# Sign of a weight through a parametric relu on ScalarE, a last value chunk on all rows, and a planner that knows TensorE's low clock

## The chip, the cores and the metric

The kernel runs on one core of one Trainium2 chip. The metric is the device time of one execution in microseconds (us), lower is better. TensorE is called PE here, VectorE DVE, ScalarE ACT, GpSimd POOL, and SyncE, which issues the DMAs, SP.

## What is computed

A masked attention over 4 batches, 8 heads, 576 positions and head size 64, then two layers of an MLP (2304 tokens, 512 to 2048 to 512):

```python
scores = scale * np.matmul(q, k.transpose(0, 1, 3, 2))
thresh = np.max(scores, axis=-1, keepdims=True) - tau
scores = np.where(scores >= thresh, scores, -1000000000.0)
attn = np.exp(scores - np.max(scores, axis=-1, keepdims=True))
attn = attn / (np.sum(attn, axis=-1, keepdims=True) + 1e-09)
x = np.matmul(attn, v)                      # then (2304, 512)
h = x @ w_in
x = (np.maximum(h, 0) + np.log1p(np.exp(-np.abs(h)))) @ w_out      # first MLP
h = x @ w_in2
out = (np.maximum(h, 0) ** 2) @ w_out2                             # second MLP
```

## The kernel before

**Stages.** The attention is cut into 32 units (`u`): two heads and half of the queries each. Four units give the 512 features of one group of 288 tokens; there are 8 groups. The first MLP works on one group at a time in 8 steps (`p`), each with 256 of the 2048 inner features; the second MLP works on 512 tokens at a time (`p` again 0 to 7). The first MLP begins when the first four units are done and runs beside the attention of the later ones; the second MLP follows.

**One unit.** `a_prep` splits q and k into a high and a low part (ACT, then POOL lines 250 and 251). `a_scores` makes the scores transposed, five chunks of 128 keys: four chunks with two heads side by side on 64 rows of PE each (line 266), the fifth with both heads' last 64 keys on 128 rows (line 271); ACT moves them to SBUF (line 274). `a_max` reduces them on DVE (lines 282 to 290) and spreads the maximum by a DMA to DRAM and back (292, 293). `a_soft` subtracts, masks (DVE, lines 300 and 302) and takes the exponential (ACT, line 303). `a_out` multiplies with the values on PE: for each of two heads four chunks on all 128 rows (line 314) and the last chunk on that head's 64 rows only (line 315); the chunk tensor `vp` has zeros in the rows of the other head. Each of these fp32 matmuls is two MATMUL records in the trace. ACT copies the results (316, 317), DVE divides (319 to 322). `x_split` splits the group's features (328, 329).

**MLP.** `m1_up` (lines 338 to 340, three matmuls per product on 288 columns), the softplus on ACT and DVE (348 to 351), a split (356, 357), `m1_down` (369 to 371). The second MLP has the same lines 338 to 340 and then 458 to 466 and 478 to 480.

**Weights.** They come as 64-bit floats: 64 pieces of 128x512 words, 32 for each MLP, in `Weights.load`. ACT scales the high word into `t` (line 227), which loses nothing but the sign; POOL multiplies the high word by zero, which leaves the sign bit (228); DVE shifts the low word and ors that sign in (229), then shifts `t` by three and ors (230); ACT rounds to the high part (231); POOL subtracts for the low part (232). The first MLP's 32 pieces have two buffers (`wraw`, `wt`), the second's three, and a buffer is loaded again when its last reader is done.

**Order.** Nothing is issued in the order of the code: `Plan` collects operations with an engine, an assumed duration, reads, writes and a key (the due step), and `emit` lists them by a simple model in which each engine takes the ready operation with the lowest key, operations with `lock=True` exclude POOL's, and costs such as a DMA's rate are constants of the class. That list is what each engine then executes strictly in order. One plan covers the attention with the first MLP, a second one the rest.

Of the kernel before, what the change touches and what calls it, by code (L numbers as in the profile page):

```python
# [12 lines left out]
AF = mybir.ActivationFunctionType  # L13
ALU = mybir.AluOpType
# [12 lines left out]
LAG = 13  # L27
EARLY = 6
PREPDVE = 1
WLEAD, W2LAG = 7, 3  # L30
GPOOL = range(8, 56)
DOWN = 2.0 ** -20


def f32(ap):
    return ap.bitcast(F32)


class Plan:
# [5 lines left out]

    SYNC, AFTER_PE, DRAIN, DMA_START, DMA_END, BYTES_PER_NS = 200, 300, 130, 1600, 950, 350

# [19 lines left out]
    def emit(self):  # L67
# [14 lines left out]
        future, ready, events = {}, {}, []  # L82
# [15 lines left out]
        while left:  # L98
# [10 lines left out]
            while future[e] and future[e][0][0] <= t:  # L109
                _, key, i = heapq.heappop(future[e])  # L110
                heapq.heappush(ready[e], (key, i))
            _, i = heapq.heappop(ready[e])
            eng, ns, fn, deps, key, nbytes, lock = self.ops[i]
# [27 lines left out]
def kernel(ctx: ExitStack, tc: tile.TileContext, qT, kT, vp, tau, w1i, w1o, w2i, w2o, out):  # L141
# [59 lines left out]


    class Weights:
        def __init__(self, pool, n):
# [6 lines left out]
        def load(self, src, f, outw, key=None):  # L211
            s = self.i % self.n
            self.i += 1
            raw, t = self.raw[s], self.t[s]
            R, T = ("wraw", id(self), s), ("wt", id(self), s)
            p, j = divmod(f, 2)
            hi, lo = (woh, wol) if outw else (wih, wil)
            W = ("wo" if outw else "wi", p)
            if outw:
                P.add("SP", 600, lambda: SP.dma_start(raw.rearrange("p e w -> p (e w)"), src[f * 128:(f + 1) * 128, :]), [], [R], key, 1 << 19)  # L220
                hf, lf, t2 = hi[p][:, j], lo[p][:, j], t
            else:
                P.add("SP", 600, lambda: SP.dma_start(raw.rearrange("p e w -> p (e w)"), src[f]), [], [R], key, 1 << 19)
                hf, lf = (x[p][:, :, 128 * j:128 * j + 128] for x in (hi, lo))
                t2 = t.rearrange("p (k f) -> p k f", k=4)
            low, high = raw[:, :, 0], raw[:, :, 1]
            P.add("ACT", 510, lambda: ACT.mul(f32(t), f32(high), 2.0 ** -112), [R], [T], key)
            P.add("POOL", 620, lambda: POOL.tensor_scalar(f32(high), f32(high), 0.0, 1.0, op0=ALU.mult, op1=ALU.mult), [], [R], key)
            P.add("DVE", 620, lambda: DVE.scalar_tensor_tensor(out=low, in0=low, scalar=29, in1=high, op0=ALU.logical_shift_right, op1=ALU.bitwise_or), [], [R], key, lock=True)  # L229
            P.add("DVE", 620, lambda: DVE.scalar_tensor_tensor(out=t, in0=t, scalar=3, in1=low, op0=ALU.logical_shift_left, op1=ALU.bitwise_or), [R], [T], key, lock=True)  # L230
            P.add("ACT", 510, lambda: ACT.copy(hf, f32(t2)), [T], [W], key)
            P.add("POOL", 1230, lambda: POOL.tensor_tensor(lf, f32(t2), f32(hf), op=ALU.subtract), [T], [W], key)

# [19 lines left out]
    def a_scores(u, key):  # L253

        st, ST = st_t[u % 3], ("st", u % 3)
        half = [slice(0, 64), slice(64, 128)]
        ops = [(k_h, q_h), (k_l, q_h), (k_h, q_l)]
        QK = ["k_h", "k_l", "q_h", "q_l"]
        for c in range(5):
            banks = [(y_ps[i], ("y", i)) for i in (2 * (c % 2), 2 * (c % 2) + 1)] if u < EARLY else [(a_ps[i], ("a", i)) for i in range(2)]  # L260
            cs = slice(128 * c, 128 * c + 128)
            if c < 4:
                def mms(banks=banks, cs=cs):
                    for n, (k, q) in enumerate(ops):
                        for o in range(2):
                            PE.matmul(banks[o][0][:, :HALF], k[half[o], cs], q[half[o]], start=(n == 0), stop=(n == 2))  # L266
                P.add("PE", 590, mms, QK, [b[1] for b in banks], key + 0.1 * c)
            else:
# [7 lines left out]
    def a_max(u, key):  # L276
# [10 lines left out]
        for a in range(4):  # L287
            P.add("DVE", 175, lambda a=a: DVE.tensor_copy(mr[:, 1 + a, :18], r[32 * a:32 * a + 32].rearrange("p o b -> p (o b)")), [R], [MR], key)
        P.add("DVE", 360, lambda: DVE.tensor_reduce(mr[:, 0, :18], mr[:, 1:5, :18].rearrange("p a x -> p x a"), axis=AX.X, op=ALU.max), [], [MR], key)
# [14 lines left out]

    def a_out(u, key):
        e, E = st_t[u % 3], ("st", u % 3)
        vt, V = v_t[u % 2], ("v", u % 2)
# [3 lines left out]
        for o in range(2):  # L311
            bank, BK = a_ps[o][:, :HALF], ("a", o)
            for c in range(4):
                P.add("PE", 486, lambda c=c, o=o, bank=bank: PE.matmul(bank, vt[:, 192 * c + 64 * o:192 * c + 64 * o + 128], e[:, 5 * o + c], start=(c == 0), stop=False), [E, V], [BK], key + o)  # L314
            P.add("PE", 486, lambda o=o, bank=bank: PE.matmul(bank, vt[half[o], 768 + 128 * o:896 + 128 * o], e[half[o], 4], start=False, stop=True), [E, V], [BK], key + o)  # L315
            P.add("ACT", 310, lambda o=o, bank=bank: ACT.copy(xf[half[o]], bank[half[o]]), [BK], [XF], key + o - 0.5)
# [15 lines left out]
    def up(banks, p, xh, xl, X, ns, key):  # L332

        for j, (bank, BK) in enumerate(banks):
            f = slice(128 * j, 128 * j + 128)
            for c in range(4):
                def mms(bank=bank, c=c, f=f):
                    PE.matmul(bank, wih[p][:, c, f], xh[c], start=(c == 0), stop=False)  # L338
                    PE.matmul(bank, wih[p][:, c, f], xl[c], start=False, stop=False)  # L339
                    PE.matmul(bank, wil[p][:, c, f], xh[c], start=False, stop=(c == 3))  # L340
                P.add("PE", 3 * ns, mms, [("wi", p)] + X(c), [BK], key)

# [16 lines left out]
    def m1_down(k, key):  # L359
        g, p = divmod(k, NP)  # L360
        g_h, g_l = g_hl
        for j in range(2):
            for e in range(4):
# [4 lines left out]
                def mms(j=j, es=es, o=o, first=first, last=last):  # L368
                    PE.matmul(o, woh[p][:, j, es], g_h[j], start=first, stop=False)  # L369
                    PE.matmul(o, wol[p][:, j, es], g_h[j], start=False, stop=False)  # L370
                    PE.matmul(o, woh[p][:, j, es], g_l[j], start=False, stop=last)  # L371
                P.add("PE", 393, mms, [("wo", p), ("g_h", j), ("g_l", j)], [("y", e)], key)

# [94 lines left out]
    def m2_down(i, p, key):  # L468
        t0, n = groups[i]
        g_h, g_l = g2_hl  # L470
        for j in range(2):
            for t in range(n // 128):
# [4 lines left out]
                def mms(j=j, ts=ts, o=o, first=first, last=last):  # L477
                    PE.matmul(o, g_h[j][:, ts], woh[p][:, j], start=first, stop=False)  # L478
                    PE.matmul(o, g_h[j][:, ts], wol[p][:, j], start=False, stop=False)  # L479
                    PE.matmul(o, g_l[j][:, ts], woh[p][:, j], start=False, stop=last)  # L480
                P.add("PE", 700, mms, [("wo", p), ("g2h", j), ("g2l", j)], [("y", t)], key)
        if p == NP - 1:
# [90 lines left out]
```

## Time and profile before

| | before |
|---|---|
| median of 3 runs | 1226.22 us (1225.64 to 1227.43) |
| the profiled execution's own time | 1225.94 us |
| its span, first to last instruction | 1224.2 us |
| PE busy | 1136.5 us (93%) |
| DVE busy | 734.8 us (60%) |
| ACT busy | 647.6 us (53%) |
| POOL busy | 318.0 us (26%) |
| mean granted TensorE clock | 0.965 |

The profiled execution is within 0.3 us of the median, and 1.7 us of its time lie outside the span. A busy share is an average over stages: here it hides a first stretch in which PE waits and a long one in which it doesn't, so the views below are cut by time. In the views a granted clock of 1.00 is 2.4 GHz and 0.50 is 1.2 GHz; a number between is a mix of the two over time. MATMUL records overlap, so the distance from one start to the next says more than a record's length.

### The profile page before, as it was taken

To read this page: it belongs to the slowest core of one execution; us is meant where nothing else is said; L and a number is where in the kernel's file an instruction comes from. 1 tells how busy PE (TensorE), PEld (TensorE's weight loads), DVE (VectorE), ACT (ScalarE), POOL (GpSimd) and SP (SyncE) were. 2 spreads that over 40 slices of the span, in tenths; PEclk is the share of its full clock that TensorE was granted. 3 is DMA by queue.
4 is the path that set the end of the run, shared out by engine and by line. 5 is a ranking of instruction groups with operands and counts; after the bars stand their busy time and mean duration, and the time that the engine had idled before them with its cause. 6 is when DMAs were issued, how large, how long until landed. Compare 5 with 4: busy or idle time off the path is not lost.

```text
span 1224.2 us, 17099 instructions
## 1 busy us (share of the span) xinstructions
PE 1136.5 (93%) x6400; PEld 941.3 (77%) x6400; DVE 734.8 (60%) x1122; ACT 647.6 (53%) x1375; POOL 318.0 (26%) x294
## 2 busy tenths in 40 slices
PE   5465758999999999999999999999999999999998
PEld 3343646888888888888888889998888888888887
DVE  6888788867576675765756754689742232232232
ACT  6464655766766667666676756775532232222222
POOL 4254545122232222322222212366600000000000
PEclk9985778999999999999999999999999999999999
DMA  5343333122131121221212110655420010000000
GB/s 191 123 150 122 129 129 111 44 75 73 54 92 47 58 90 53 75 63 58 91 53 65 58 37 1 215 186 161 131 69 1 1 52 1 1 35 1 1 36 18
DMA packets 39971, 90.31 MB, mean 74 GB/s; under 512 B 6352, under 2 KB 15056, under 8 KB 39888
## 3 DMA queue, kind: packets, MB, share of 16 engines
q1 hardware_dynamic: 39888, 89.22, 22.8%
q8 instruction: 50, 0.82, 0.3%
q14 instruction: 33, 0.27, 0.1%
HBM read 79.69 MB, written 9.51 MB: 73 GB/s over the span
## 4 chain that ended last, share of the span: by engine, by line
PE 88%; DVE 5%; ACT 3%; issue 2%; DMA 1%; POOL 1%; SPq 0%; POOLq 0%; DVEq 0%; ACTq 0%
PE a_ps L314 12%; PE h_ps L338 12%; PE h_ps L339 11%; PE h_ps L340 11%; PE y_ps L369 6%; PE y_ps L479 6%; PE y_ps L478 6%; PE y_ps L480 5%; PE y_ps L371 5%; PE y_ps L370 5%; PE a_ps L266 5%; PE a_ps L315 4%; ACT st L303 1%; PE a_ps L271 1%; DVE wraw L229 1%
## 5 line engine op out<-in xcount | busy, mean ns | idle before, releaser
L314 PE MATMUL a_ps<-st,v_t 128*128 128x288 f32 x512 | 153.9, 448 | 51.8 <-ACT st L303 51.8
L357 POOL TENSOR_TENSOR g_l<-gt,g_h 128x288 fp32r<-128x288 f32 x96 | 87.4, 917 | 349.9 <-ACT g_h L356 211.4
L314 PEld LDWEIGHTS a_ps<-st,v_t 128*128 128x128 f32 x512 | 101.0, 207 | 91.8 <-ACT st L303 53.9
L369 PE MATMUL y_ps<-g_h,woh 128*128 128x288 f32 x512 | 158.7, 310 | 0.0
L338 PE MATMUL h_ps<-x_h,wih 128*128 128x288 f32 x512 | 158.0, 309 | 0.2 <-DVE gt L351 0.2
L371 PE MATMUL y_ps<-g_l,woh 128*128 128x288 f32 x512 | 151.2, 295 | 1.6 <-DVE g_l L357 1.6
L340 PE MATMUL h_ps<-x_h,wil 128*128 128x288 f32 x512 | 152.3, 297 | 0.0
L370 PE MATMUL y_ps<-g_h,wol 128*128 128x288 f32 x512 | 150.9, 295 | 0.0
L339 PE MATMUL h_ps<-x_l,wih 128*128 128x288 f32 x512 | 150.8, 295 | 0.0
L351 DVE SCALAR_TENSOR_TENSOR gt<-h_ps,a_t 128x288 f32<-128x288 f32 x128 | 57.6, 452 | 132.2 <-ACT a_t L350 127.6
L459 DVE SCALAR_TENSOR_TENSOR r<-h_ps,r 128x512 f32<-128x512 f32 (+1 forms) x80 | 50.7, 635 | 120.4 <-ACT r L458 120.4
L300 DVE TENSOR_TENSOR st<-st,mb 128x1152 f32<-128x1152 f32 (+1 forms) x128 | 120.6, 942 | 0.7
L339 PE MATMUL h_ps<-y_l,wih 128*128 128x512 f32 (+1 forms) x320 | 120.0, 375 | 0.0
L338 PE MATMUL h_ps<-y_h,wih 128*128 128x512 f32 (+1 forms) x320 | 119.2, 372 | 0.0
L340 PE MATMUL h_ps<-y_h,wil 128*128 128x512 f32 (+1 forms) x320 | 118.7, 371 | 0.0
L466 DVE TENSOR_TENSOR g_l<-r,g_h 128x512 fp32r<-128x512 f32 (+1 forms) x80 | 54.0, 675 | 104.2 <-ACT g_h L465 104.1
L465 ACT CAST g_h<-r 128x512 fp32r<-128x512 f32 (+1 forms) x80 | 46.2, 578 | 131.2 <-PE y_ps L479 128.4
L479 PE MATMUL y_ps<-wol,g_h 128*128 128x512 f32 x288 | 114.1, 396 | 0.0
L478 PE MATMUL y_ps<-woh,g_h 128*128 128x512 f32 x288 | 114.1, 396 | 0.0
L480 PE MATMUL y_ps<-woh,g_l 128*128 128x512 f32 x288 | 114.0, 396 | 0.0
L458 ACT ACTIVATE r<-h_ps 128x512 f32<-128x512 f32 (+1 forms) x80 | 44.2, 553 | 129.9 <-PE h_ps L340 127.7
L369 PEld LDWEIGHTS y_ps<-g_h,woh 128*128 128x128 f32 x512 | 96.3, 188 | 16.7 <-issue 15.6
(92 smaller groups left out, 2534.8 us busy)
## 6 DMA issues: line engine op xcount, KB each, us to landing
v_t<-in_vp SPq DMA_DIRECT2D x32, 512.0 KB
k_r<-in_kT SPq DMA_DIRECT2D x32, 320.0 KB
mb<-m_d SPq DMA_DIRECT2D x32, 288.0 KB
wraw<-in_w1i SPq DMA_DIRECT2D x16, 512.0 KB
wraw<-in_w1o SPq DMA_DIRECT2D x16, 512.0 KB
wraw<-in_w2i SPq DMA_DIRECT2D x16, 512.0 KB
wraw<-in_w2o SPq DMA_DIRECT2D x16, 512.0 KB
q_r<-in_qT SPq DMA_DIRECT2D x32, 144.0 KB
```

The source lines that it names most:

```text
L300: DVE.tensor_tensor(st[p0:p1, a:a + n], st[p0:p1, a:a + n], mb[p0:p1, o:o + 1].to_broadcast([p1 - p0, n, HALF]), op=ALU.subtract),
L314: P.add("PE", 486, lambda c=c, o=o, bank=bank: PE.matmul(bank, vt[:, 192 * c + 64 * o:192 * c + 64 * o + 128], e[:, 5 * o + c], start=(c = ...
L338: PE.matmul(bank, wih[p][:, c, f], xh[c], start=(c == 0), stop=False)
L339: PE.matmul(bank, wih[p][:, c, f], xl[c], start=False, stop=False)
L340: PE.matmul(bank, wil[p][:, c, f], xh[c], start=False, stop=(c == 3))
L357: P.add(eng, ns, lambda j=j: e.tensor_tensor(g_hl[1][j], gt_t[j], f32(g_hl[0][j]), op=ALU.subtract), [("gt", j), ("g_h", j)], [("g_l", j)] ...
L369: PE.matmul(o, woh[p][:, j, es], g_h[j], start=first, stop=False)
L370: PE.matmul(o, wol[p][:, j, es], g_h[j], start=False, stop=False)
L371: PE.matmul(o, woh[p][:, j, es], g_l[j], start=False, stop=last)
L478: PE.matmul(o, g_h[j][:, ts], woh[p][:, j], start=first, stop=False)
L479: PE.matmul(o, g_h[j][:, ts], wol[p][:, j], start=False, stop=False)
L480: PE.matmul(o, g_l[j][:, ts], woh[p][:, j], start=False, stop=last)
```

## The change

Four things change.

- The sign: ACT's multiplication becomes a parametric relu with the same scale and a slope of -2^32 for negative inputs, so that the sign arrives in an exponent bit that the later shift by three moves to the top. POOL's multiplication is gone, and DVE's first operation is a plain shift of one input (`tensor_scalar`), no longer a shift and or of two.
- The last chunk of values is multiplied on all 128 rows for both heads instead of 64 rows each; the zeros in `vp` take the other head out.
- A weight piece is written and read under its own name (`j` added), so that the first half of a step's work doesn't wait for the second piece.
- The planner: scores and output of the first six units cost 1.8 times as much, the DMA rate is 300 instead of 350 bytes per ns, the four small copies of line 288 are locked against POOL, some durations are new. `LOOK` is an empty table, and with it the new branch in `emit` never takes an operation early.

```diff
+NCOLD, COLD = 6, 1.8
-    SYNC, AFTER_PE, DRAIN, DMA_START, DMA_END, BYTES_PER_NS = 200, 300, 130, 1600, 950, 350
+    SYNC, AFTER_PE, DRAIN, LOOK, DMA_START, DMA_END, BYTES_PER_NS = 200, 300, 130, {}, 1600, 950, 300
...
-            W = ("wo" if outw else "wi", p)
+            W = ("wo" if outw else "wi", p, j)
...
-            P.add("ACT", 510, lambda: ACT.mul(f32(t), f32(high), 2.0 ** -112), [R], [T], key)
-            P.add("POOL", 620, lambda: POOL.tensor_scalar(f32(high), f32(high), 0.0, 1.0, op0=ALU.mult, op1=ALU.mult), [], [R], key)
-            P.add("DVE", 620, lambda: DVE.scalar_tensor_tensor(out=low, in0=low, scalar=29, in1=high, op0=ALU.logical_shift_right, op1=ALU.bitwise_or), [], [R], key, lock=True)
-            P.add("DVE", 620, lambda: DVE.scalar_tensor_tensor(out=t, in0=t, scalar=3, in1=low, op0=ALU.logical_shift_left, op1=ALU.bitwise_or), [R], [T], key, lock=True)
+            P.add("ACT", 560, lambda: ACT.activation(f32(t), f32(high), AF.Prelu, scale=2.0 ** -112, alpha=-2.0 ** 32), [R], [T], key)
+            P.add("DVE", 330, lambda: DVE.tensor_scalar(low, low, 29, None, op0=ALU.logical_shift_right), [], [R], key, lock=True)
+            P.add("DVE", 610, lambda: DVE.scalar_tensor_tensor(out=t, in0=t, scalar=3, in1=low, op0=ALU.logical_shift_left, op1=ALU.bitwise_or), [R], [T], key, lock=True)
...
-                P.add("PE", 590, mms, QK, [b[1] for b in banks], key + 0.1 * c)
+                P.add("PE", 590 * cold, mms, QK, [b[1] for b in banks], key + 0.1 * c)
...
-            P.add("DVE", 175, lambda a=a: DVE.tensor_copy(mr[:, 1 + a, :18], r[32 * a:32 * a + 32].rearrange("p o b -> p (o b)")), [R], [MR], key)
+            P.add("DVE", 175, lambda a=a: DVE.tensor_copy(mr[:, 1 + a, :18], r[32 * a:32 * a + 32].rearrange("p o b -> p (o b)")), [R], [MR], key, lock=True)
...
-            P.add("PE", 486, lambda o=o, bank=bank: PE.matmul(bank, vt[half[o], 768 + 128 * o:896 + 128 * o], e[half[o], 4], start=False, stop=True), [E, V], [BK], key + o)
+            P.add("PE", 486 * cold, lambda o=o, bank=bank: PE.matmul(bank, vt[:, 768 + 128 * o:896 + 128 * o], e[:, 4], start=False, stop=True), [E, V], [BK], key + o)
...
-                P.add("PE", 3 * ns, mms, [("wi", p)] + X(c), [BK], key)
+                P.add("PE", 3 * ns, mms, [("wi", p, j)] + X(c), [BK], key)
...
-                P.add("PE", 393, mms, [("wo", p), ("g_h", j), ("g_l", j)], [("y", e)], key)
+                P.add("PE", 393, mms, [("wo", p, j), ("g_h", j), ("g_l", j)], [("y", e)], key)
```

What the planner makes of it, at three places. In these lists a row is the line in the respective file, the operation, what it writes and reads, and the shape. New line numbers: 229 is 237 now, 230 is 238, 282 is 291, 232 is 240, 250 and 251 are 258 and 259.

DVE at the start, before: the first two weight pieces, the maximum of unit 0 (`m_156`) and that of unit 1 (`m_157`).

```order
L229 SCALAR_TENSOR_TENSOR wraw_181<-wraw_181 128x512
L230 SCALAR_TENSOR_TENSOR wt_183<-wt_183,wraw_181 128x512
L282 TENSOR_REDUCE m_156<-st_153 128x81
L229 SCALAR_TENSOR_TENSOR wraw_182<-wraw_182 128x512
L283 TENSOR_REDUCE r_158<-m_156 128x18
L230 SCALAR_TENSOR_TENSOR wt_184<-wt_184,wraw_182 128x512
L286 TENSOR_TENSOR r_158<-r_158,m_156 64x9 x2
L288 COPY mr_160<-r_158 32x18 x2
L229 SCALAR_TENSOR_TENSOR wraw_181<-wraw_181 128x512
```

The same place now.

```order
L237 TENSOR_SCALAR wraw_181<-wraw_181 128x512
L238 SCALAR_TENSOR_TENSOR wt_183<-wt_183,wraw_181 128x512
L237 TENSOR_SCALAR wraw_182<-wraw_182 128x512
L238 SCALAR_TENSOR_TENSOR wt_184<-wt_184,wraw_182 128x512
L291 TENSOR_REDUCE m_156<-st_153 128x81
L292 TENSOR_REDUCE r_158<-m_156 128x18
L295 TENSOR_TENSOR r_158<-r_158,m_156 64x9
L237 TENSOR_SCALAR wraw_181<-wraw_181 128x512
L295 TENSOR_TENSOR r_158<-r_158,m_156 64x9
```

The shift has one input and stands in front of the maximum for both pieces; the piece behind it is done before the maximum begins.

POOL at the start, before: the sign (228), the low parts of k and q (251, 250) and of the first weights (232).

```order
L228 TENSOR_SCALAR wraw_181<-wraw_181 128x512
L228 TENSOR_SCALAR wraw_182<-wraw_182 128x512
L251 TENSOR_TENSOR k_l<-k_r,k_h 128x640
L250 TENSOR_TENSOR q_l<-q_r,q_h 128x288
L232 TENSOR_TENSOR wil_77<-wt_183,wih_69 128x4x128
L228 TENSOR_SCALAR wraw_181<-wraw_181 128x512
```

The same place now.

```order
L240 TENSOR_TENSOR wil_77<-wt_183,wih_69 128x4x128
L258 TENSOR_TENSOR q_l<-q_r,q_h 128x288
L259 TENSOR_TENSOR k_l<-k_r,k_h 128x640
L240 TENSOR_TENSOR wil_77<-wt_184,wih_69 128x4x128
L240 TENSOR_TENSOR wol_93<-wt_183,woh_85 128x512
```

Only subtractions are left on POOL, and the first weight's low part stands ahead of q's and k's.

PE where the second MLP's first step (512 columns) is mixed into the first MLP's last ones (288 columns), before:

```order
L338 MATMUL h_ps_67<-x_h_124,wih_75 128x288
L339 MATMUL h_ps_67<-x_l_128,wih_75 128x288
L340 MATMUL h_ps_67<-x_h_124,wil_83 128x288
L338 MATMUL h_ps_6448<-y_h_6451,wih_70 128x512
L339 MATMUL h_ps_6448<-y_l_6452,wih_70 128x512
```

The same place now.

```order
L348 MATMUL h_ps_67<-x_h_124,wih_73 128x288
L349 MATMUL h_ps_67<-x_l_128,wih_73 128x288
L350 MATMUL h_ps_67<-x_h_124,wil_81 128x288
L348 MATMUL h_ps_6416<-y_h_6419,wih_70 128x512
L349 MATMUL h_ps_6416<-y_l_6420,wih_70 128x512
```

The first matmul that needs the second MLP's weights stands two steps of the first MLP earlier (its weight piece is `wih_73`, not `wih_75`).

## Rows read from the trace of the kernel before

**Rows 1.** Windows of core 0: us, busy by engine (count), PE clock, DMA share.
```profile
0.00:195.20 195.20, 115.84 (x531) 83.62 (x531) 157.09 (x215) 108.05 (x224) 92.67 (x82) 0.80 0.42 138
...
205.70:734.00 528.30, 527.80 (x3447) 445.53 (x3447) 357.09 (x607) 352.25 (x803) 136.51 (x136) 1.00 0.21 65
734.00:796.00 62.00, 60.36 (x434) 57.96 (x433) 32.76 (x53) 40.61 (x90) 18.52 (x18) 1.00 0.33 108
796.00:1160.00 364.00, 364.00 (x1623) 296.54 (x1622) 160.56 (x202) 124.44 (x213) 62.98 (x54) 1.00 0.17 53
```

**Rows 2.** Chain of waits, 190 to 210 us: start, us, what.
```profile
197.72 4.21 PE a_ps L314 x8
```

**Rows 3.** Waits of PE, 0 to 195.2 us: us in total, times, longest.
```profile
PE a_ps L314 <- ACT st L303: 48.0, 5, 17.3
```

**Rows 4.** Timeline of PE, output of two units: start, us, line, tiles, shape, count.
```profile
227.55 2.59 PE L314 MATMUL a_ps<-st,v_t 128*128 128x288 f32 x10
230.07 0.75 PE L315 MATMUL a_ps<-st,v_t 64*128 64x288 f32 x2
...
249.06 3.56 PE L314 MATMUL a_ps<-st,v_t 128*128 128x288 f32 x14
252.54 0.75 PE L315 MATMUL a_ps<-st,v_t 64*128 64x288 f32 x2
...
254.58 0.40 PE L369 MATMUL y_ps<-g_h,woh 128*128 128x288 f32 x1
254.82 0.29 PE L370 MATMUL y_ps<-g_h,wol 128*128 128x288 f32 x1
254.95 0.29 PE L371 MATMUL y_ps<-g_l,woh 128*128 128x288 f32 x1
```

**Rows 5.** Groups by line and shape, PE, 206 to 800 us.
```profile
L315 PE MATMUL a_ps<-st,v_t 64*128 64x288 f32 x100 | 37.5, 455 | 0.0
```

**Rows 6.** Timeline of PE's weight loads at the second of these units.
```profile
248.92 3.23 PEld L314 LDWEIGHTS a_ps<-st,v_t 128*128 128x128 f32 x14
252.54 0.29 PEld L315 LDWEIGHTS a_ps<-st,v_t 64*128 64x128 f32 x2 [0.39 <-issue]
```

**Rows 7.** Groups by line, DVE, 0 to 195.2 us: busy, mean ns | idle before, releaser.
```profile
L230 DVE SCALAR_TENSOR_TENSOR wt<-wt,wraw 128x512 uint32<-128x512 uint32 x28 | 23.9, 858 | 0.3
...
L229 DVE SCALAR_TENSOR_TENSOR wraw<-wraw 128x512 uint32<-128x512 uint32 x29 | 22.8, 788 | 19.6 <-POOL wraw L228 19.5
...
L288 DVE COPY mr<-r 32x18 f32<-32x18 f32 x32 | 12.5, 391 | 0.7
L286 DVE TENSOR_TENSOR r<-r,m 64x9 f32<-64x9 f32 x16 | 6.6, 413 | 0.2
...
L357 DVE TENSOR_TENSOR g_l<-gt,g_h 128x288 fp32r<-128x288 f32 x6 | 2.5, 436 | 0.0
```

**Rows 8.** Waits of DVE, 0 to 195.2 us.
```profile
DVE wraw L229 <- POOL wraw L228: 19.5, 12, 4.1
```

**Rows 9.** Groups by line, POOL, 0 to 195.2 us.
```profile
L228 POOL TENSOR_SCALAR wraw<-wraw 128x512 f32<-128x512 f32 x30 | 30.1, 1005 | 47.1 <-ACT wt L227 47.1
```

**Rows 10.** Timelines of DVE and POOL: operations alone, and side by side.
```profile
18.12 1.40 DVE L288 COPY mr<-r 32x18 f32<-32x18 f32 x2
18.23 1.27 POOL L232 TENSOR_TENSOR wil<-wt,wih 128x512 fp32r<-128x512 f32 x1
...
11.55 0.65 POOL L228 TENSOR_SCALAR wraw<-wraw 128x512 f32<-128x512 f32 x1 [0.58 <-ACT wt L227]
...
19.56 0.69 DVE L229 SCALAR_TENSOR_TENSOR wraw<-wraw 128x512 uint32<-128x512 uint32 x1
...
44.26 0.16 DVE L288 COPY mr<-r 32x18 f32<-32x18 f32 x1
```

**Rows 11.** Groups by line, ACT, 0 to 245 us.
```profile
L227 ACT ACTIVATE wt<-wraw 128x512 f32<-128x512 f32 x32 | 21.4, 669 | 11.2 <-DMA wraw<-in_w1o 7.0 <-POOL wol L232 3.2 <-DMA wraw<-in_w1i 1.0
...
L165 ACT ACT_TABLE_LOAD x1 | 1.3, 1283 | 0.7 <-PEq L565 0.7
```

More of the change, by code (lines that the diff above doesn't have):

```diff
@@ L111, in emit @@
                 heapq.heappush(ready[e], (key, i))
-            _, i = heapq.heappop(ready[e])
+            soon = [f for f in future[e] if f[0] <= t + self.LOOK.get(e, 0) and f[1] < LAG and (not ready[e] or f[1:] < ready[e][0])]
+            if soon:
+                f = min(soon, key=lambda f: f[1:])
+                future[e].remove(f)
+                heapq.heapify(future[e])
+                t, i = f[0], f[2]
+            else:
+                _, i = heapq.heappop(ready[e])
             eng, ns, fn, deps, key, nbytes, lock = self.ops[i]
@@ L226, in load @@
             low, high = raw[:, :, 0], raw[:, :, 1]
-            P.add("ACT", 510, lambda: ACT.mul(f32(t), f32(high), 2.0 ** -112), [R], [T], key)
-            P.add("POOL", 620, lambda: POOL.tensor_scalar(f32(high), f32(high), 0.0, 1.0, op0=ALU.mult, op1=ALU.mult), [], [R], key)
-            P.add("DVE", 620, lambda: DVE.scalar_tensor_tensor(out=low, in0=low, scalar=29, in1=high, op0=ALU.logical_shift_right, op1=ALU.bitwise_or), [], [R], key, lock=True)
-            P.add("DVE", 620, lambda: DVE.scalar_tensor_tensor(out=t, in0=t, scalar=3, in1=low, op0=ALU.logical_shift_left, op1=ALU.bitwise_or), [R], [T], key, lock=True)
+            P.add("ACT", 560, lambda: ACT.activation(f32(t), f32(high), AF.Prelu, scale=2.0 ** -112, alpha=-2.0 ** 32), [R], [T], key)
+            P.add("DVE", 330, lambda: DVE.tensor_scalar(low, low, 29, None, op0=ALU.logical_shift_right), [], [R], key, lock=True)
+            P.add("DVE", 610, lambda: DVE.scalar_tensor_tensor(out=t, in0=t, scalar=3, in1=low, op0=ALU.logical_shift_left, op1=ALU.bitwise_or), [R], [T], key, lock=True)
             P.add("ACT", 510, lambda: ACT.copy(hf, f32(t2)), [T], [W], key)
-            P.add("POOL", 1230, lambda: POOL.tensor_tensor(lf, f32(t2), f32(hf), op=ALU.subtract), [T], [W], key)
+            P.add("POOL", 1240, lambda: POOL.tensor_tensor(lf, f32(t2), f32(hf), op=ALU.subtract), [T], [W], key)
     def a_load(u, key):
@@ L253, in a_scores @@
     def a_scores(u, key):
+        cold = COLD if u < NCOLD else 1
         st, ST = st_t[u % 3], ("st", u % 3)
@@ L305, in a_out @@
     def a_out(u, key):
+        cold = COLD if u < NCOLD else 1
         e, E = st_t[u % 3], ("st", u % 3)
@@ L313, in a_out @@
             for c in range(4):
-                P.add("PE", 486, lambda c=c, o=o, bank=bank: PE.matmul(bank, vt[:, 192 * c + 64 * o:192 * c + 64 * o + 128], e[:, 5 * o + c], start=(c == 0), stop=False), [E, V], [BK], key + o)
-            P.add("PE", 486, lambda o=o, bank=bank: PE.matmul(bank, vt[half[o], 768 + 128 * o:896 + 128 * o], e[half[o], 4], start=False, stop=True), [E, V], [BK], key + o)
+                P.add("PE", 486 * cold, lambda c=c, o=o, bank=bank: PE.matmul(bank, vt[:, 192 * c + 64 * o:192 * c + 64 * o + 128], e[:, 5 * o + c], start=(c == 0), stop=False), [E, V], [BK], key + o)
+            P.add("PE", 486 * cold, lambda o=o, bank=bank: PE.matmul(bank, vt[:, 768 + 128 * o:896 + 128 * o], e[:, 4], start=False, stop=True), [E, V], [BK], key + o)
             P.add("ACT", 310, lambda o=o, bank=bank: ACT.copy(xf[half[o]], bank[half[o]]), [BK], [XF], key + o - 0.5)
@@ L480, in mms @@
                     PE.matmul(o, g_l[j][:, ts], woh[p][:, j], start=False, stop=last)
-                P.add("PE", 700, mms, [("wo", p), ("g2h", j), ("g2l", j)], [("y", t)], key)
+                P.add("PE", 700, mms, [("wo", p, j), ("g2h", j), ("g2l", j)], [("y", t)], key)
         if p == NP - 1:
```

## The prediction

> **What bounds the kernel now.** I read the windows first. From 205.7 us on PE is busy without a break at the full clock: 527.80 of 528.30 us up to 734, and all 364.00 us from 796 to 1160; between 734 and 796 it loses 62.00 - 60.36 = 1.6 us [rows 1]. What PE has to do there sets the time, and an operation of another engine counts only if PE has to wait for it. The first 195.2 us are different: PE works 115.84 us at a mean clock of 0.80, and DVE is the fullest engine with 157.09 us, ahead of ACT's 108.05 and POOL's 92.67 [rows 1]. PE's longest wait there is for the exponentials, 48.0 us in 5 times [rows 3], and an exponential follows DVE's mask. The marker between the two stretches is the output of unit 6, which starts at 197.72 us [rows 2]. So the sum has two terms: what PE saves behind the marker, and how much earlier the marker comes.
>
> The sum goes by the profiled execution: 1225.94 us, of which 1224.2 are its span. Its time is 0.3 us below the median of the three runs, which I add at the end.
>
> **The change part by part: full rows.** Line 315 has 64 rows, line 314 has 128. Its price is read from starts. A block of 10 records of line 314 lasts 230.07 - 227.55 = 2.52 us until line 315 begins, a block of 14 lasts 252.54 - 249.06 = 3.48 [rows 4]; so one more record costs (3.48 - 2.52) / 4 = 0.24 us. The whole unit of 16 + 4 records takes 254.58 - 249.06 = 5.52 us. At 0.24 each, 20 records would take 4.80, so the two switches to 64 rows and back cost 0.72. The first record behind the unit pays too: line 369 to line 370 takes 0.24, while 370 to 371 takes 0.13 [rows 4]. Together 0.83; since starts are rounded, I count 0.8 us a unit. With 128 rows line 315 has line 314's shape on the same tiles, so it should cost what that costs. Behind the marker there are 100 records of line 315 [rows 5], at 4 a unit 25 units: 25 x 0.8 = 20 us, all on the path, since PE never waits there. What hides it: nothing. What is next late: in 205.7 to 734 DVE is busy 357.09 and ACT 352.25 of 528.30 us [rows 1], so both keep up when PE needs 20 us less. I take 20. The ends are 17 (0.72 less rounding, without the record behind) and 21.
>
> A second look at the weight loads: the loads of line 314 run in one stream of 14 beside the matmuls, from 248.92 on, and the load of line 315 waits 0.39 us at its switch [rows 6]. The Trainium skill's page "TensorE: Matmul & The Clock Gate" (Part 3, The mechanism) states that a weight load overlaps with running matmuls only when the row group differs. By that rule full rows would keep every load waiting and the 20 us would shrink towards nothing; the rows show the opposite order, a stream at equal rows and a wait at the change of rows, and I follow them.
>
> **The start: less on DVE and POOL.** What must be over before the marker is the mask of unit 6, DVE's seventh operation of line 302, at about 195 us. The list of DVE's operations up to there has 28 weight pieces before and 30 in the changed kernel. Four terms.
>
> (a) DVE stood idle 19.5 us in 12 waits for POOL's sign [rows 8]. POOL's operation alone takes 0.65 us [rows 10], so at least 12 x 0.65 = 7.8 us go; the most is 19.5. The rest of each wait was ACT's scaling, for which POOL itself waited 47.1 us [rows 9], and DVE's second operation still needs that. I take the middle, 14.
>
> (b) Line 229 took 22.8 us [rows 7]. Its replacement has one input. No row shows a wide one-input operation of DVE with SBUF on both sides. One end is the two-input shift alone, 0.69 us, the other is what a tiny copy costs, 0.16 [rows 10]. I take the copy's 0.16 plus half of the difference, 0.43, because one input leaves half the reading: 30 x 0.43 = 12.9, a gain of 9.9. The ends are 30 x 0.69 = 20.7 (a gain of 2.1) and 30 x 0.16 = 4.8 (18.0).
>
> (c) DVE's operations get longer when POOL works. Two copies of line 288 that take 0.16 each took 1.40 us beside a subtraction of POOL of 1.27 [rows 10]. Over the stretch, line 288 has 32 x (0.391 - 0.16) = 7.4 us of this, line 286 (as small) 16 x (0.413 - 0.16) = 4.0, line 230 28 x (0.858 - 0.69) = 4.7 [rows 7, 10], together 16.1. The sign is 30.1 of POOL's 92.67 busy us [rows 1, 9], so a third, 5.2, goes; the ends are 0 and 8. Against it stand the new shifts: if each is held up like a copy of line 288, 30 x 0.23 = 6.9 us come back, if none is, 0. I take 4.6. The Trainium skill's page "SBUF — State Buffer" (SBUF: two separate sides) speaks against the change here: a one-input DVE operation in a two-port mode and a POOL operation exclude each other for the whole instruction. The copies of line 288 bear it out [rows 10]; with the upper 6.9 the sum would be 2.3 us worse.
>
> (d) The planner puts more in front of the marker: two more second operations, 2 x 0.69 = 1.4, and the six subtractions of line 357, 6 x 0.436 = 2.6 [rows 7, 10], which before POOL's stretch stood behind. Together 4.0 lost. They save nothing later, because PE sets the time there.
>
> Sum: -14 - 9.9 - 5.2 + 4.6 + 4.0 = -20.5, taken as **20 us** earlier. The ends are -19.5 - 18.0 - 8 + 0 + 4 = -41 and -7.8 - 2.1 - 0 + 6.9 + 4 = +1. I count one us less on DVE as one us earlier, since DVE is 157 of 195 us busy and much of its idle time is the 19.5 of (a).
>
> **Edits taken at nothing.** ACT's parametric relu is costed like the scaling it replaces, 669 ns for the same shape [rows 11]; ACT idles 195.2 - 108.05 = 87 us in the first stretch, which covers some tens of ns on each. The seven units before the marker save on line 315 too, but there PE waits for DVE; 0 to 5. The half-step names release matmuls that PE, in its fixed order, reaches later anyway. In the second MLP's weights (32 pieces) DVE and POOL get lighter, but PE is full there; at most the 1.6 us of [rows 1] come back. PE now meets the first 512-column matmul two steps of the first MLP earlier. If its weight is not ready, all behind it on PE waits, for about the making of one piece: 0.67 + 0.43 + 0.69 + 0.67 + 1.27 = 3.7 us [rows 10, 11]. I take 0 between -1.6 and +4. The other constants only move the order.
>
> **The sum.** 1225.9 - 20 - 20 = 1185.9 in the profiled execution, with 0.3 for the median **1186 us**.
>
> **The rivals.**
>
> 1. The wait moves to ACT. DVE's second operation follows ACT's relu, and ACT executes in order behind copies that wait for PE; then (a) is no gain but a wait under another name, and the shifts fight POOL. For it: POOL's 47.1 us of waiting for ACT [rows 9]. Against it: ACT is busy only 108 of 195 us. The start gains 3: 1226 - 20 - 3 = 1203.
>
> 2. All of the start's good end: the waits vanish, the shifts are cheap, and PE, less often idle, keeps its full clock: 1226 - 20 - 41 = 1165. For it: the clock of 0.80 leaves something to win. Against it: DVE's chain of maximum, DMA, mask and exponential stays as long.
>
> 3. The full rows bring nothing: what line 315 loses is not the switch but the chunk itself, or the loads stall as in the page's rule. 1226 - 20 = 1206. [rows 6] speak against it.
>
> 4. Slower: the relu is not in the activation tables that ACT has loaded, and each piece brings a table load before it and one behind it. One takes 1.28 us [rows 11], so 30 pieces cost 30 x 2 x 1.28 = 77 us on ACT ahead of the marker. ACT idles 87 us there, so part is hidden; the change becomes slower once more than the 40 us of gains lie on the path. With three quarters of it, 58, the time is 1226 + 58 - 40 = 1244. Against it: the list of the changed kernel's instructions has one table load, at the start.
>
> **How the numbers follow.** Forecast, 1175 to 1197: 0.62. Rival 1: 0.18. Rival 2: 0.10. Rival 3: 0.05. Rival 4: 0.03. About the same time as before, by several small losses in the start: 0.02. The range holds the forecast, rivals 1 and 3 and the near part of rival 2: 1168 to 1206 leaves out the rest of rival 2, rival 4 and the tails. A measurement of this kernel tells 0.2% (2.5 us) from no change: faster 0.95, same 0.02, slower 0.03.
>
> **What would show it.** In the profile after: no switch in the outputs, a unit in 4.8 us and its next record 0.13 us later; the output of unit 6 at about 178 us; the shift near 0.43 us; no wait of DVE for POOL's sign, and less than 6 us of new waits of its second operation for ACT; PE without a break behind the marker. It is wrong if PE's outputs keep their 5.5 us, if the marker stays near 198, or if PE waits in the second MLP.

## The result and the profile after

The changed kernel takes 1176.7 us in the median (1176.56 to 1177.44), where the kernel before takes 1226.8 in the same measurement: a ratio of 0.9591, with a 95% interval of 0.9574 to 0.9608. That is 50 us less, within the range of 1168 to 1206; the forecast was 1186, nine us too slow. The span fell from 1224.2 to 1174.9 us, by 49.3. Both terms of the sum can be found in the trace, but the gain of the start is made of other parts than the prediction gave it.

The windows of the changed kernel, in the columns of [rows 1] and with the borders moved along:

```profile
0.00:171.40 171.40, 109.50 (x533) 85.15 (x534) 154.32 (x225) 111.82 (x227) 69.82 (x55) 0.83 0.51 163
181.70:686.90 505.20, 505.20 (x3421) 449.97 (x3420) 351.51 (x599) 349.61 (x795) 134.44 (x132) 1.00 0.22 67
686.90:749.00 62.10, 62.10 (x452) 60.91 (x451) 34.66 (x59) 43.64 (x98) 15.86 (x15) 1.00 0.37 123
749.00:1110.00 361.00, 361.00 (x1603) 293.73 (x1602) 147.87 (x196) 120.50 (x205) 35.89 (x26) 1.00 0.16 51
```

From 181.7 us on PE has no break up to 1110: 505.20 of 505.20 us in the long window, and the 1.6 us lost at 734 to 796 before are gone too. Ahead of it DVE is still the fullest engine, 154.32 of 171.4 us. Its busy time fell by only 2.8 us against [rows 1]; its idle time fell from 38.1 to 17.1.

The marker, the output of unit 6, in PE's timeline (start, us, line, count), then the output of unit 9, which answers to [rows 4], and its weight loads, which answer to [rows 6]:

```profile
173.89 4.22 PE L324 MATMUL a_ps<-st,v_t 128*128 128x288 f32 x12
...
242.36 3.07 PE L324 MATMUL a_ps<-st,v_t 128*128 128x288 f32 x12
245.26 0.65 PE L325 MATMUL a_ps<-st,v_t 128*128 128x288 f32 x2
245.75 1.13 PE L324 MATMUL a_ps<-st,v_t 128*128 128x288 f32 x4
246.72 0.65 PE L325 MATMUL a_ps<-st,v_t 128*128 128x288 f32 x2
246.99 0.51 PE L379 MATMUL y_ps<-g_h,woh 128*128 128x288 f32 x1
247.34 0.30 PE L380 MATMUL y_ps<-g_h,wol 128*128 128x288 f32 x1
```

```profile
243.81 1.16 PEld L324 LDWEIGHTS a_ps<-st,v_t 128*128 128x128 f32 x5
245.02 0.43 PEld L325 LDWEIGHTS a_ps<-st,v_t 128*128 128x128 f32 x2
245.51 0.92 PEld L324 LDWEIGHTS a_ps<-st,v_t 128*128 128x128 f32 x4
```

The marker came 23.8 us earlier (197.7 to 173.9). The new line 325 follows line 324 at the same pace, and its load no longer shows the wait of 0.39 us.

DVE ahead of the marker, answering to [rows 7] (by line: count | busy, mean ns | idle before) and, as the waits of the same stretch, to [rows 8]:

```profile
L238 DVE SCALAR_TENSOR_TENSOR wt<-wt,wraw 128x512 uint32<-128x512 uint32 x32 | 28.2, 885 | 1.9 <-ACT wt L236 1.4
...
L297 DVE COPY mr<-r 32x18 f32<-32x18 f32 x32 | 16.2, 505 | 0.6
L237 DVE TENSOR_SCALAR wraw<-wraw 128x512 uint32<-128x512 uint32 x32 | 15.4, 482 | 2.5 <-DMA wraw<-in_w1i 2.3
```

```profile
DVE qsc L175 <- DMA tau_t<-in_tau: 4.0, 1, 4.0
DVE m L291 <- ACT st L283: 3.1, 4, 1.1
DVE wraw L237 <- DMA wraw<-in_w1i: 2.3, 1, 2.3
DVE k_l L259 <- ACT k_h L257: 1.4, 1, 1.4
DVE wt L238 <- ACT wt L236: 1.4, 3, 0.7
```

No wait for POOL is left, and none of more than 4.0 us. The shift costs 482 ns on average where the old operation cost 788; but the second operation (858 before) and above all the copies (391 before) became longer.

### The profile page after: what moved, and what is told of

It is laid out like the page before. It is cut to its first block, busy times and chain, and to the rows that moved or that the text cites. A ratio compares the mean times of both kernels' runs of the same rounds, so it can differ in the third digit from the quotient of the medians.

```text
span 1174.9 us, 16931 instructions
## 1 busy us (share of the span) xinstructions
PE 1108.9 (94%) x6400; PEld 951.7 (81%) x6400; DVE 712.3 (61%) x1122; ACT 647.6 (55%) x1375; POOL 260.3 (22%) x230
## 3 DMA queue, kind: packets, MB, share of 16 engines
q1 hardware_dynamic: 39888, 89.22, 24.3%
## 4 chain that ended last, share of the span: by engine, by line
PE 85%; DVE 8%; DMA 2%; ACT 2%; issue 2%; SPq 0%; ACTq 0%
PE h_ps L348 12%; PE h_ps L349 11%; PE h_ps L350 11%; PE a_ps L324 9%; PE y_ps L379 6%; PE y_ps L488 6%; PE y_ps L489 6%; PE y_ps L490 6%; PE y_ps L380 6%; PE y_ps L381 5%; PE a_ps L275 5%; DVE st L309 2%; PE a_ps L325 2%; DMA wraw<-in_w1i 1%; DVE st L311 1%
## 5 line engine op out<-in xcount | busy, mean ns | idle before, releaser
L324 PE MATMUL a_ps<-st,v_t 128*128 128x288 f32 x512 | 145.3, 430 | 22.8 <-ACT st L312 22.8
L367 POOL TENSOR_TENSOR g_l<-gt,g_h 128x288 fp32r<-128x288 f32 x96 | 90.4, 949 | 328.0 <-ACT g_h L366 201.1
L379 PE MATMUL y_ps<-g_h,woh 128*128 128x288 f32 x512 | 161.5, 315 | 0.0
L309 DVE TENSOR_TENSOR st<-st,mb 128x1152 f32<-128x1152 f32 (+1 forms) x128 | 118.2, 923 | 1.8 <-DMA mb<-m_d 1.1
L348 PEld LDWEIGHTS h_ps<-x_h,wih 128*128 128x128 f32 x512 | 97.6, 191 | 14.6 <-DVE gt L361 6.2
```

Of the source, the lines that this page charges most:

```text
L309: DVE.tensor_tensor(st[p0:p1, a:a + n], st[p0:p1, a:a + n], mb[p0:p1, o:o + 1].to_broadcast([p1 - p0, n, HALF]), op=ALU.subtract),
L324: P.add("PE", 486 * cold, lambda c=c, o=o, bank=bank: PE.matmul(bank, vt[:, 192 * c + 64 * o:192 * c + 64 * o + 128], e[:, 5 * o + c], sta ...
L367: P.add(eng, ns, lambda j=j: e.tensor_tensor(g_hl[1][j], gt_t[j], f32(g_hl[0][j]), op=ALU.subtract), [("gt", j), ("g_h", j)], [("g_l", j)] ...
```

## The experiments

Theory A: the sum's reading, full rows behind the marker and the sign ahead of it. Theory B: the order of work, which the prediction took at nothing, carries the start. Where a line number differs by one or more, it is the same line of the code in that kernel.

For the kernels that tell A and B apart, and those at a fixed order, the start of the output of unit 6 (the marker) and of unit 8 is read from PE's timeline, and DVE's busy and idle time from the window that ends 2.5 us ahead of the marker, as in [rows 1] (us):

| kernel | marker | DVE busy | DVE idle | unit 8 | span |
|---|---|---|---|---|---|
| before | 197.7 | 157.1 | 38.1 | 249.1 | 1224.2 |
| rows alone | 192.0 | 157.5 | 32.0 | 241.8 | 1199.9 |
| sign alone | 186.5 | 154.5 | 29.5 | 231.7 | 1206.3 |
| order alone | 196.6 | 169.4 | 24.7 | 241.0 | 1212.3 |
| sign and rows, old order | 183.8 | 156.3 | 25.0 | 227.5 | 1183.8 |
| changed kernel | 173.9 | 154.3 | 17.1 | 220.0 | 1174.9 |
| changed, no factor for the low clock | 184.4 | 153.0 | 28.9 | 233.2 | 1187.9 |
| changed, two-input shift | 180.2 | 160.9 | 16.8 | 225.6 | 1180.9 |
| changed, POOL work beside | 181.1 | 161.1 | 17.5 | 226.6 | 1181.5 |
| changed, POOL's sign back | 194.5 | 168.4 | 23.6 | 239.5 | 1205.9 |

With the order alone PE has 587 records in that window, where the other kernels have 531 to 544: more of the later work stands ahead of the marker, so of that kernel only unit 8 and the span compare.

**Rows alone.**

```diff
-PE.matmul(bank, vt[half[o], 768 + 128 * o:896 + 128 * o], e[half[o], 4], start=False, stop=True)
+PE.matmul(bank, vt[:, 768 + 128 * o:896 + 128 * o], e[:, 4], start=False, stop=True)
```

> The kernel before with the full rows of line 315 alone. Theory (the two switches of rows cost 0.8 us a unit, all on the path behind the marker): 25 x 0.8 = 20 us less, some 1206 us; the marker, the output of unit 6, stays near 198 us, since PE waits for DVE in front of it, and a unit's output takes 4.8 us instead of 5.5. Rival (the chunk itself is what costs, or the weight loads stall at equal rows): 1224 to 1227 us and an output of 5.5 us.

Measured: 1201.4 us, ratio 0.9785 (0.9769 to 0.9802), 26 us less (differences in us between kernels are taken from the ratios, here and below). From the output of unit 7 to that of unit 31, 24 units, PE needs 516.2 us before (227.6 to 743.8) and 497.4 here (221.1 to 718.5): 18.8 us or 0.78 a unit, as the theory has it, and the rival is out. But the marker did not stay: it came 5.7 us earlier. DVE's waits and ACT's ahead of it, of this kernel, and then ACT's of the kernel before, show why:

```profile
DVE wraw L229 <- POOL wraw L228: 13.5, 11, 4.1
```

```profile
ACT xf L316 <- PE a_ps L315: 25.4, 11, 5.1
```

```profile
ACT xf L316 <- PE a_ps L315: 30.5, 11, 5.0
```

The waits of [rows 8] fell from 19.5 to 13.5 us with nothing changed in the sign. ACT waits 25.4 us for the outputs where it waited 30.5, its scaling of the next weight stands behind that, POOL's sign behind the scaling and DVE behind the sign. A shorter output shortens the whole chain. DVE's direct wait for the outputs, at the division (line 319), stayed at 7.6 us in both kernels.

**Sign alone, order alone, and both of sign and rows in the old order.** The first puts the three new lines of `Weights.load` into the kernel before, the second everything of the diff but these and the rows, the third is the first with the full rows.

> The kernel before with the weight's new operations and their costs alone (parametric relu, one-input shift, no sign on POOL); rows and the planner's constants stay old. Theory A (the sign carries the gain of the start): DVE's 19.5 us of waits for POOL are gone, the marker comes 17 to 25 us earlier, 1201 to 1210 us. Rival B (the order carries it): the waits go to ACT or to SP's loads, the marker moves by less than 6 us, 1220 to 1227 us. Rival C (each needs the other): about 10 us, 1214 to 1219.

> The kernel before with the planner's part of the change alone (low clock of the first six units, 300 bytes per ns, locked copies, names by half step); sign and rows stay old. Theory A: DVE still waits about 20 us for POOL's sign in the first 195 us, 1222 to 1231 us. Rival B: the old sign under the new order loses its waits too, 1203 to 1210 us.

> The changed kernel with the planner's constants, the locks and the names of before, that is sign and full rows together. Theory A (the order is worth little): 1176 to 1184 us, no more than 7 us above the changed kernel. Rival B (the order carries the start): 1195 to 1203 us, the gain of the full rows alone. If the parts simply add, its gain is that of the rows alone plus that of the sign alone.

Measured: the sign alone 1208.8 us, ratio 0.9854 (0.983 to 0.9877), 18 us less; the order alone 1212.4, 0.9877 (0.9861 to 0.9892), 15 less; sign and rows 1186.2, 0.9665 (0.965 to 0.968), 41 less. Neither A nor B holds alone: the order is worth 15 us by itself and 9 on top of the other two. The sign alone reached the time of its theory A, but by another way: the marker came 11.2 us earlier, not 17 to 25. The order alone and the old order both fell between their theories, and the gains of rows and sign nearly add (26 and 18 against 41). The waits of DVE ahead of the marker in the kernel before, beside the one in [rows 8], then with the sign alone, and then one of these in the timelines of PE, DVE and PE again:

```profile
DVE d L319 <- ACT rb L317: 7.6, 3, 4.0
```

```profile
DVE d L318 <- ACT rb L316: 12.1, 6, 4.2
DVE qsc L167 <- DMA tau_t<-in_tau: 4.0, 1, 4.0
DVE wt L229 <- ACT wt L227: 3.5, 4, 1.2
```

```profile
79.75 4.21 PE L313 MATMUL a_ps<-st,v_t 128*128 128x288 f32 x8 [5.95 <-ACT st L302]
83.89 1.21 PE L314 MATMUL a_ps<-st,v_t 64*128 64x288 f32 x2
85.03 2.21 PE L313 MATMUL a_ps<-st,v_t 128*128 128x288 f32 x8
87.16 0.75 PE L314 MATMUL a_ps<-st,v_t 64*128 64x288 f32 x2
```

```profile
88.79 0.48 DVE L318 TRANSPOSE_TENSOR_REDUCE d<-rb 128x9 f32<-128x288 f32 x1 [4.24 <-ACT rb L316]
...
91.95 2.88 DVE L301 SCALAR_TENSOR_TENSOR st<-st,thr 128x2592 f32<-128x2592 f32 x1
```

```profile
97.37 4.21 PE L313 MATMUL a_ps<-st,v_t 128*128 128x288 f32 x8 [5.29 <-ACT st L302]
```

The 19.5 us of waits for POOL are gone, but DVE's idle time fell by 8.6 only, because others grew: the wait of a unit's division for its output (line 319 before, 318 here) from 7.6 to 12.1, and 3.5 us are new, of the second operation for ACT. This is half of rival 1. The timeline shows one such wait. PE produces an output from 79.75 to about 87.9, the first ten records at the low clock in 5.28 us (granted 0.52), the other ten at the full clock in 2.9. DVE's row has the division of that unit ahead of the mask of the next, so it stands 4.24 us, the mask begins at 91.95 and the next output at 97.37, for which PE had waited 5.29 us.

**No factor for the low clock.** `COLD` is 1 instead of 1.8 in the changed kernel.

> The changed kernel without the factor for the low clock (1 instead of 1.8 in the planner); the other constants, locks and names stay. Theory: the factor is what the order brings, since sign and rows without the new order lose 9 us: about 1186 us, with the marker near 184 us. Rival: another constant brings it, 1175 to 1179 us.

Measured: 1189.5 us, ratio 0.9695 (0.9678 to 0.9712), 13 us slower than the changed kernel and 3 to 4 slower than with the whole order undone, though those two intervals touch. The marker is at 184.4, as the theory has it. DVE's wait for the outputs is back:

```profile
DVE d L329 <- ACT rb L327: 10.1, 5, 3.5
```

So the factor is what the order brings, and the wait shows how: with the output of the first units costed at 1.8 times, the planner puts the division behind work that DVE can do meanwhile. Without the factor the division of unit 0 stands ahead of the mask of unit 1 and waits 3.5 us (it begins at 51.1, the mask at 54.6); with it the mask stands first (51.2) and the division follows at 54.1 without a wait, as do the other five ahead of the marker.

A rival is the clock itself, since the start's mean clock is 0.73 here and 0.83 in the changed kernel. The single executions speak against it. Without the factor, two had a mean clock of 0.957 over the whole execution and took 1190.0 and 1190.3 us, two had 0.971 and took 1188.7 and 1189.1, which is still some 12 us above the changed kernel at 0.973. The rate of 300 and the names by half step were not tried alone.

**The parts of the sign, at a fixed order.** Three kernels that issue every other operation exactly as the changed kernel does:

```diff
# two inputs
-DVE.tensor_scalar(low, low, 29, None, op0=ALU.logical_shift_right)
+DVE.scalar_tensor_tensor(out=low, in0=low, scalar=29, in1=high, op0=ALU.logical_shift_right, op1=ALU.bitwise_and)
# POOL beside, issued with the first 30 relus; idle is a view of the last step's weights
+POOL.tensor_scalar(idle, ident.unsqueeze(1).to_broadcast([128, 4, 128]), 0.0, 1.0, op0=ALU.mult, op1=ALU.mult)
# sign back, issued with every relu, and DVE's old operation behind it
+POOL.tensor_scalar(f32(high), f32(high), 0.0, 1.0, op0=ALU.mult, op1=ALU.mult)
-DVE.tensor_scalar(low, low, 29, None, op0=ALU.logical_shift_right)
+DVE.scalar_tensor_tensor(out=low, in0=low, scalar=29, in1=high, op0=ALU.logical_shift_right, op1=ALU.bitwise_or)
```

> The changed kernel in exactly its order, but DVE's first operation of a piece reads two inputs again, the low and the high word, and ands them (the last three bits of a weight's 24-bit mantissa are partly lost; nothing else changes). It prices term (b) alone. Theory: the two-input form takes 0.69 us undisturbed where the shift's median is 0.415, so 32 pieces ahead of the marker bring 32 x 0.27 = 8.8 us and the time goes from 1176.7 to about 1185. Rival: DVE's 17 us of idle time ahead of the marker takes it in, 1177 to 1179 us.

> The changed kernel in its order, with 30 extra operations of POOL of the removed sign's size and 8-byte output step at the places where the sign stood, on a tile that nobody waits for (weights of the last step, which their own piece overwrites later). It prices term (c), the contention, without a wait of DVE for POOL. Theory: about 30 x 0.65 = 20 us more of POOL beside DVE lengthen DVE's operations by 5 us ahead of the marker, 1182 us (upper end of the forecast 8, 1185). Rival: no price, 1176 to 1178 us.

> The changed kernel in its order, with POOL's sign back in place on the high word and DVE's first operation as the old shift and or, which waits for it; ACT keeps the parametric relu. Everything that the sign's path cost, (a), (b) and (c), at the new order. The forecast's terms give 14 + 9.9 + 5.2 - 4.6 = 24.5: 1201 us. Rival: the runs so far leave 49 - 26 (rows alone) - 15 (order alone) = 8 us for the sign in the new order: 1185 us. What is above the sum of the two runs on (b) and on (c) is the wait (a).

Measured: two inputs 1183.4 us, ratio 0.9647 (0.9627 to 0.9668), 7 us slower than the changed kernel; POOL beside 1182.2, 0.9638 (0.9621 to 0.9654), 6 slower; the sign back 1208.3, 0.9847 (0.983 to 0.9865), 31 slower and above the 1201 of its theory. The rows that carry this: DVE's first operation with two inputs; POOL's extra operation; and, with the sign back, DVE's waits ahead of the marker and PE's waits behind 225 us.

```profile
L237 DVE SCALAR_TENSOR_TENSOR wraw<-wraw 128x512 uint32<-128x512 uint32 x32 | 25.0, 781 | 2.7 <-DMA wraw<-in_w1i 2.5
```

```profile
L241 POOL TENSOR_SCALAR wol<-ident 128x512 fp32r<-128x512 f32 x30 | 22.7, 758 | 0.9
```

```profile
DVE wraw L237 <- POOL wraw L236: 11.3, 11, 3.8
```

```profile
PE h_ps L348 <- DVE gt L361: 6.5, 5, 2.3
PE y_ps L490 <- DVE g_l L476: 1.6, 1, 1.6
```

Of the marker's 20.6 us, 6.3 belong to the second input, 7.2 to POOL's work, and, if the parts add, the rest, 7.1, to the wait. DVE's idle time took in none of the added work: it is 16.8 and 17.5 us in the first two (17.1 in the changed kernel), while the busy time rose by 6.6 and 6.8; with the sign back it rose by 6.5 beside 14.1 of work. So one us added to DVE's row is one us of the marker, as the prediction counted; whether one us taken off it counts as much, the copies below tell. The other 11 us of the third kernel are lost where the second MLP's weights are made, 8.1 of them in the waits of PE shown above, from 753 to 854 us. Most of these (6.5 us) name DVE's softplus (line 361), which stands in DVE's row among the weight pieces; from 735 to 870 us DVE waits 12.9 us for POOL's sign, in 14 times, and the softplus stands behind these waits. The list was drawn up for the short making of a weight. The order alone, whose list knows the old sign, has 1.2 us of waits of PE behind 200 us and none there.

**The copies.** Ahead of the marker the changed kernel's four small copies of a unit are longer than before. Two kernels: no lock on them in the planner; or all four in one group on ACT.

```diff
-P.add("DVE", 175, lambda a=a: DVE.tensor_copy(...), [R], [MR], key, lock=True)
+P.add("ACT", 800, lambda: [ACT.copy(mr[:, 1 + a, :18], r[32 * a:32 * a + 32].rearrange("p o b -> p (o b)")) for a in range(4)], [R], [MR], key)
```

> The changed kernel with the four small copies (line 297) no longer locked against POOL in the planner. In the changed kernel they take 505 ns each ahead of the marker, in the kernel before 391. Theory: the lock doesn't keep them apart on the chip and only pushes them back in DVE's row, so it is worth nothing: 1175 to 1179 us. Rival: it shortens what waits behind them, and without it the time rises by 3 us or more.

> The changed kernel with the four small copies of a unit (line 297) on ACT in one group. Ahead of the marker DVE is busy 154 of 171 us, 16.2 of these with the copies; ACT 112. Theory (DVE's work ahead of the marker sets the time, one for one): up to 16 us less, 1161 to 1168 us. Rival (the chain from the maximum over DMA and mask to the output sets it): the copies wait on ACT behind copies that wait for PE, 1175 to 1185 us.

Measured: without the lock 1178.8 us, ratio 0.9604 (0.9591 to 0.9617), not told apart from the changed kernel, so the lock is worth nothing that shows. On ACT 1170.4, 0.9533 (0.9519 to 0.9547): the fastest kernel of this study, some 7 us below the changed one. Rows of DVE's window ahead of the marker and of ACT's copies:

```profile
0.00:171.50 171.50, 115.51 (x564) 90.52 (x565) 145.16 (x196) 120.69 (x265) 76.23 (x55) 0.84 0.52 165
```

```profile
L296 ACT COPY mr<-r 32x18 f32<-32x18 f32 x32 | 6.5, 203 | 0.9 <-DVE r L295 0.7
```

ACT does in 6.5 us what cost DVE 16.2, 203 ns a copy. Both expectations were wrong in part: DVE's busy time fell by 9 and unit 8 came 5.3 us earlier, not 16. The marker itself stayed (174.0), so DVE's row alone doesn't set it any more: in nearly the same window DVE's idle time rose from 17.1 to 26.3, 5.5 of it waiting for the DMA of weights (2.3 before the copies moved) and 4.3 for ACT at the softplus (1.2 before).

**Seven units, and both steps together.** `NCOLD` is 7 instead of 6, alone and with the copies on ACT.

> The changed kernel with the planner's factor 1.8 for seven units instead of six; in the changed kernel the output of the seventh still begins at the low clock. Theory (the factor works by putting DVE's division of a unit behind the end of its output on PE): a wait of the seventh unit's division goes, 1 to 4 us less, 1173 to 1176 us. Rival: no wait is left there, and the order changes by chance, 1176 to 1182 us.

> Both of the last two steps in the changed kernel: the four small copies on ACT and the factor for seven units. Alone they gave 0.9533 and 0.9563 of the kernel before, where the changed kernel has 0.9591. Theory (both take time off DVE's row ahead of the marker, and the gains add): 0.9591 - 0.0058 - 0.0028 = 0.9505, about 1166.5 us. Rival (each sets a new order, and only one of them counts): 0.953 to 0.957, 1169 to 1174 us.

Measured: 1173.2 us, 0.9563 (0.955 to 0.9576), some 3 us below the changed kernel, though the intervals touch. The theory's wait is gone: in the changed kernel the seventh unit's division, behind the marker, has the row below, and with seven units DVE has no such wait there, since the next unit's mask stands first.

```profile
DVE d L329 <- ACT rb L327: 3.7, 1, 3.7
```

Both together took 1174.8 us, ratio 0.9566 (0.9549 to 0.9582), no better than the factor alone and slower than the copies alone. The gains don't add: each edit makes the planner draw up another order, and a few us come and go with it; which part of the order took the gain back was not looked for.

## Why the prediction was right, and where it was not

The three parts, stacked in the order rows, sign, order (us earlier, from the table above):

| | marker | unit 8 | span |
|---|---|---|---|
| full rows | 5.7 | 7.3 | 24.3 |
| sign, on top | 8.2 | 14.3 | 16.1 |
| order, on top | 9.9 | 7.5 | 8.9 |
| together | 23.8 | 29.1 | 49.3 |

The sum's two terms are found as 23.8 us ahead of the marker (20 forecast) and 18.8 from the output of unit 7 to that of unit 31 (20 forecast). The remaining 6.6 lie outside both: 4.4 between the outputs of units 6 and 7 and 2.2 behind the output of unit 31, and the break of 1.6 us that is gone (at 785.6 in the kernel before) is part of the 2.2. What the 4.4 are made of was not taken apart.

- **Full rows behind the marker: right.** 25 x 0.8 = 20 was forecast; 24 units give 18.8, 0.78 each. The detail was off and cancelled: the unit takes 246.99 - 242.36 = 4.63 us, not 4.80, and its next record follows after 0.35, not 0.13; together 4.98 against 5.76 in [rows 4]. Rival 3 is out by the rows alone (0.9785). Two loads of line 325 begin at 245.02 and the next load at 245.51, 0.24 us each and without a wait. The trace thus doesn't agree with the Trainium skill's page "TensorE: Matmul & The Clock Gate" (Part 3, The mechanism), by which a load overlaps with running matmuls only when the row group differs.
- **Full rows ahead of the marker: wrong.** "0 to 5", taken as 0, because PE waits for DVE there. It was 5.7, where 0.8 for each of the six outputs ahead of the marker makes 4.8 (somewhat more at the low clock, where the starts of two records lie 0.60 to 0.64 us apart at a switch instead of 0.48): they lie on the path, since DVE waits for ACT's copies of them by way of the sign (19.5 us before, 13.5 with the rows alone). The waits of [rows 8] should have been followed one releaser further back than ACT.
- **(a), waits for POOL: 14 forecast; the mechanism right, the net smaller.** In the old order the sign took 8.6 us of idle time off DVE; at the new order putting the sign back costs 7.1, just under the lower end of 7.8. The rest reappeared, mostly as waits for ACT, until the order removed it.
- **(b), the shift: right.** 9.9 forecast. Undisturbed it takes 0.416 us in the median (the 43 of 64 that no operation of POOL overlaps by more than 0.05 us) against 0.43; (788 - 482) x 30 is 9.2 us of DVE's time. The two-input form cost 6.3 at the marker, since its first operation took 9.6 us more and the copies, by chance of what POOL did beside them, 5.3 less.
- **(c), contention: inside its ends, but too cheap, and wrong for what is left.** 5.2 was forecast for 30.1 us of POOL's work, 0.17 us for each; measured are 7.2 for 22.7, 0.32 us for each. But neither the second operation (858 to 885 ns) nor the copies (391 to 505) became shorter: POOL's subtractions now fall on them instead.
- **(d) and the constants: wrong.** Of the 4.0 that (d) counts as lost, the two second operations are there (30 ahead of the mask of unit 6 instead of 28), but the six subtractions stood ahead of the marker before, too: [rows 7] has them, 2.5 us, and it is 2.7 now. And "the other constants only move the order": the order gave 8 to 10 us, by the factor for the low clock. This is the step that failed. The prediction read nowhere how long DVE waits for outputs at its division, though 7.6 us of such waits stood next to [rows 8].
- **Edits at nothing: right.** The relu takes 674 ns against 669 [rows 11], with one table load of 1283 ns as before, so rival 4 is out. The second MLP gave back its 1.6 us.

That the start's 20 came so near to 23.8 is in part luck, because its misses have both signs: the sign's terms (24.5 together) were taken 4 us too high at the new order (20.6 at the marker) and 16 too high at the old one (8.2 on top of the rows), while the order and the rows of the start stood at nothing or at a loss. On DVE's row the forecast has 6.5 us less busy time and 14 less idle time; measured are 2.8 and 21.0. Rival 1 was half right of the sign alone: waits for ACT took the place of part of those for POOL, but the marker still came 11.2 us earlier, not 3, and the order removed these waits.

Rival 2 hoped for something from the clock of 0.80. With two inputs the start's mean clock is 0.73, with POOL beside 0.83, and the marker is the same within 1 us. Single executions with two inputs agree: at a mean clock of 0.958 and 0.959 they took 1182.7 and 1182.6 us, at 0.971 and 0.973 1184.3 and 1184.0. So this difference of the granted clock moved the time by less than 2 us.

## What to carry to other kernels

When an in-order engine waits, follow the wait back through every releaser to the work that is really late: removing the last link alone turns it into a wait for the link before. Where a planner draws up the order, its durations are part of the change, and one wrong by a factor (here the outputs at the low clock) is worth as much as an operation. And an edit that changes an order is to be priced at a fixed order too, or its parts can't be told from the luck of the new list.

## What the runs showed of the hardware

A stretched DVE operation is stretched by POOL far more than the averages of [rows 7] tell. Splitting the changed kernel's operations, over the whole span, by whether an operation of POOL overlaps them by more than 0.05 us gives medians of 416 ns alone and 1058 beside POOL for the one-input shift, 685 and 1130 for the second operation, 165 and 1170 for the small copies, while ACT's relu keeps 675 and 670. The timelines of DVE and POOL show the shift both ways:

```profile
91.21 1.72 DVE L237 TENSOR_SCALAR wraw<-wraw 128x512 uint32<-128x512 uint32 x1
...
94.08 0.43 DVE L237 TENSOR_SCALAR wraw<-wraw 128x512 uint32<-128x512 uint32 x1
```

```profile
91.12 1.53 POOL L259 TENSOR_TENSOR k_l<-k_r,k_h 128x640 fp32r<-128x640 f32 x1
```

The first shift begins with POOL's subtraction under way and ends 0.28 us after it (92.93 against 92.65); the second has DVE for itself. Which of the two begins first decides. Of the 22 shifts that meet an operation of POOL at all, seven began ahead of it and took 0.37 to 0.43 us, as alone; 15 began behind it, and 13 of these ended 0.28 to 0.29 us after POOL's record did (one 0.36 after it, and one was not held up). This fits the Trainium skill's page "SBUF — State Buffer" (SBUF: two separate sides), by which a one-input DVE operation in a two-port mode and one of POOL exclude each other for a whole instruction; that the shift runs in such a mode no row here shows. So DVE's terms are better read as two durations and the number of meetings that POOL begins than as a mean.
